# Mish feed-forward layer on one core: the first product of three row blocks done jointly on one weight load

## The chip, the core and the metric

The kernel runs on one core of one Trainium2 chip. The metric is the device time of one execution in microseconds (us). Three runs give 104.45, 105.22 and 105.36 us; the median, 105.22 us, is the time before.

## What is computed

```python
def reference(x, w1, b1, w2):          # x [1, 2048, 512], w1 [512, 1792], w2 [1792, 512], bfloat16
    h = jnp.einsum("bsd,df->bsf", x, w1) + b1
    sp = jnp.log1p(jnp.exp(-jnp.abs(h))) + jnp.where(h > 0, h, jnp.zeros_like(h))
    act = h * jnp.tanh(sp)             # mish(h)
    return jnp.einsum("bsf,fd->bsd", act, w2)
```

## The kernel before

The 2048 rows of x are worked in four blocks of 512 rows (blocks 0 to 3, the index `s`). Each block goes through two products.

**First product** (`mm1`, with its matmuls in `mm1_step`, L176). For each of FT = 14 column tiles `f` of w1 (128 columns each), KT = 4 matmuls `k` accumulate 128 values of h by the 512 rows of the block in one bank of `ps`. The weights are the tile `w1_sb[:, k, f]`; the moving operand is `xT[:, k, rows of the block]`, x transposed. After the fourth matmul ScalarE's `mish` (L159) adds the bias, applies Mish and writes `a_sb[:, f, rows of the block]`.

**Second product** (`mm2`, with its matmuls in `mm2_step`, L198). For each output tile `i` of 128 rows (16 in all, four to a block), 14 matmuls accumulate 128 rows by 512 output columns in one bank. The weights are pieces of `a_sb`, the moving operand is w2. `put` lets VectorE copy the bank to `o_sb` (L204) and SP store it (L207). The last tile is done in two pieces, of 384 and 128 columns, and the second is stored from ScalarE's queue.

Each `nc.tensor.matmul` call is two instructions on TensorE: a weight load (LDWEIGHTS, on the row PEld of the profile) and the matmul (MATMUL, on the row PE).

`ps` has eight banks of 512 float32 columns. `free[bank]` holds the instruction that last read the bank (a copy or a mish); the first matmul into a bank waits for it. Semaphore waits already known to be fulfilled are left out by `Stream.wait`. In blocks 1 to 3 the first product rotates over banks 4 to 7 and the second over 0 to 3:

```python
for f in range(FT):
    mm1(s, f, 4 + f % 4)
for i in range(starts[s] // P, starts[s + 1] // P):
    if i < S // P - 1:
        mm2(i, 0, D, i % 4)
```

Block 0 is handled apart, because it runs while the weights arrive: half of its rows are transposed by TensorE, the matmuls of its first eight tiles `f` are split by rows and ordered by the arrival of w1, and its second product uses banks `(i + 2) % 4`. Eight matmuls on constants ahead of it keep TensorE running until the data is there. The transposed x of blocks 1 to 3 (`xT`) comes by three transposing transfers, the last of the loads on SP's queue; the stores of the output follow on the same queue. Blocks 1 to 3 then run one after another: first product, second product, next block. Every engine works its instructions in the order in which they are written.

Of the kernel before, what the change touches and what calls it, by code (L numbers as in the profile page):

```python
# [5 lines left out]
P = 128  # L6
SQ = 32
WARM = (512,) * 5 + (256,) * 2 + (128,)
BLOCKS = (512, 512, 512, 512)
# [23 lines left out]
def bass_standalone__dense_activation_mish__prompt_kernel(  # L33
# [12 lines left out]
    _, S, D = x.shape  # L46
    F = w1.shape[1]
    KT, FT = D // P, F // P
# [4 lines left out]
    starts = [sum(BLOCKS[:i]) for i in range(len(BLOCKS) + 1)]  # L53
    OPEN = 8
    N0 = BLOCKS[0] // P

    with ExitStack() as es:
        def sb(name, shape, t):
            return es.enter_context(nc.sbuf_tensor(name, shape, t))

        x_nat = sb("x_nat", [P, 2, D], BF)
        xT = sb("xT", [P, KT, S], BF)
        w1_sb = sb("w1_sb", [P, KT, F], BF)
# [8 lines left out]
        ps = es.enter_context(nc.psum_tensor("ps", [P, 8, 512], F32))  # L72

        def sem(name):
            return es.enter_context(nc.semaphore(name))

        sp = Stream(nc.sync, None)
        pe = Stream(nc.tensor, sem("c_pe"))
        dve = Stream(nc.vector, sem("c_dve"))
        act = Stream(nc.scalar, sem("c_act"))  # L80
# [42 lines left out]
        for s in range(1, len(BLOCKS)):  # L123
            lo, hi = starts[s], starts[s + 1]
# [31 lines left out]
        def mish(s, f, bank, t_mm):  # L156
            n = BLOCKS[s]
            act.wait(t_b1c, t_mm)
            t = act.mark(act.eng.activation(a_sb[:, f, starts[s]:starts[s + 1]], ps[:, bank, 0:n], ACT.Mish,  # L159
                                            bias=b1_sb[:, f:f + 1]))  # L160
            t_mish[s, f] = t
            free[bank] = [t]

        def mm1_step(s, f, k, bank, js=None):

            n = BLOCKS[s]
            lo, hi = (0, n) if js is None else (js[0] * P, (js[-1] + 1) * P)
            first = k == 0 and lo == 0
            if first:
                pe.wait(*free[bank])  # L170
            pe.wait(t_w1[k, f])
            if s:
                pe.wait(t_xT[s])
            else:
                pe.wait(*[t_cp[j, k] for j in (js or range(N0))])
            return nc.tensor.matmul(ps[:, bank, lo:hi], w1_sb[:, k, f * P:(f + 1) * P],  # L176
                                    xT[:, k, starts[s] + lo:starts[s] + hi], start=first, stop=(k == KT - 1 and hi == n))

        def mm1(s, f, bank):
            for k in range(KT):  # L180
                mm = mm1_step(s, f, k, bank)
            mish(s, f, bank, pe.mark(mm))
# [10 lines left out]
        def mm2_step(i, f, lo, hi, bank):  # L193
            s = max(b for b in range(len(BLOCKS)) if starts[b] <= i * P)
            if f == 0:
                pe.wait(*free[bank])
            pe.wait(t_w2[f], t_mish[s, f])
            return nc.tensor.matmul(ps[:, bank, 0:hi - lo], a_sb[:, f, i * P:(i + 1) * P], w2_sb[:, f, lo:hi],  # L198
                                    start=(f == 0), stop=(f == FT - 1))

        def put(i, lo, hi, bank, t_mm, q=sp):
            nonlocal n_out
            dve.wait(t_mm)
            t = dve.mark(nc.vector.tensor_copy(o_sb[:, i, lo:hi], ps[:, bank, 0:hi - lo]))  # L204
            free[bank] = [t]
            q.wait(t)
            q.eng.dma_start(rows(i)[:, lo:hi], o_sb[:, i, lo:hi]).then_inc(s_out, 16)  # L207
            n_out += 1

        def mm2(i, lo, hi, bank, q=sp):  # L210
            for f in range(FT):
                mm = mm2_step(i, f, lo, hi, bank)
            put(i, lo, hi, bank, pe.mark(mm), q)
# [3 lines left out]
        def first(fs, js, ks, last=False):  # L217
            for k in ks:
                for f in fs:
                    mm = mm1_step(0, f, k, (4 + f) % 8, js)  # L220
                    if last and k == KT - 1:
                        mish(0, f, (4 + f) % 8, pe.mark(mm))
# [19 lines left out]

        for i in range(N0):
            mm2(i, 0, D, (i + 2) % 4)
        for s in range(1, len(BLOCKS)):
            for f in range(FT):
                mm1(s, f, 4 + f % 4)
            for i in range(starts[s] // P, starts[s + 1] // P):
                if i < S // P - 1:
                    mm2(i, 0, D, i % 4)  # L250
                else:
                    mm2(i, 0, D - P, i % 4)
                    mm2(i, D - P, D, (i + 1) % 4, act)
        sp.eng.wait_ge(s_out, 16 * n_out)


# [26 lines left out]
```

## Time and profile before

| | |
|---|---|
| median of three runs | 105.22 us (104.45 to 105.36) |
| time of the profiled execution | 104.7 us |
| its span, first to last instruction | 103.4 us |
| TensorE matmuls (PE) busy | 100.3 us, 97% of the span |
| TensorE weight loads (PEld) busy | 49.0 us, 47% |
| ScalarE (ACT) busy | 39.2 us, 38% |
| VectorE (DVE) busy | 13.3 us, 13% |
| mean granted TensorE clock | 1.000 |

The profile is of one execution. Its timelines give an instruction's start (us from the start of the span), its duration, engine, line and operation, then what it writes and reads, the shape and a count; in brackets stands the idle time of the engine just before, and what ended it. A row can merge several instructions of one kind, and its duration is then that of the whole stretch. Groups of instructions give busy time and mean duration (ns), then idle time before them. The windows give the busy time of each engine within a stretch, with the number of instructions, then the granted clock, the DMA engines' share and GB/s. Matmuls overlap their successors, so the duration of one (379 ns at 512 columns) is longer than the step from one to the next. A few matmul records are missing from the trace. The profile shortens names: `w_sb` is w1_sb or w2_sb, `b_sb` is b1_sb.

### The profile page before, as it was taken

What the parts mean: (1) busy time and instruction counts of PE and PEld (TensorE: products, weight loads), DVE (VectorE), ACT (ScalarE), POOL (GpSimd) and SP (SyncE); (2) the same over time, 40 slices, a digit from 0 to 9 for tenths busy, and PEclk for the clock granted to TensorE, in tenths of its full rate; (3) what the DMA queues carried; (4) which work ended last, traced back from release to release, by engine and by line L of the source; (5) the groups of instructions that cost most, each with busy time, mean ns of one, the idle gap of its engine ahead of it and who ended that gap; (6) DMA issues with size and microseconds to landing.
All of it is one profiled execution on the core that took longest, in us unless ns stands there. A gap on an engine that the chain in (4) does not pass through costs nothing.

```text
span 103.4 us, 1142 instructions
## 1 busy us (share of the span) xinstructions
PE 100.3 (97%) x497; PEld 49.0 (47%) x506; DVE 13.3 (13%) x26; ACT 39.2 (38%) x59; POOL 0.4 (0%) x5
## 2 busy tenths in 40 slices
PE   7999999999999999999999999999999999999992
PEld 2788444444444444444444444444444444444462
DVE  1212000211220000022220000022201000020223
ACT  4300999100037777100007777400006777700000
POOL 1000000000000000000000000000000000000000
PEclk9999999999999999999999999999999999999999
DMA  2999999991110000011011000001111000001111
GB/s 40 390 276 370 361 240 207 200 206 51 51 51 0 0 0 6 0 51 50 1 51 51 0 0 3 6 0 51 51 51 51 0 0 0 0 0 57 51 51 51
DMA packets 12833, 7.94 MB, mean 77 GB/s; under 512 B 7836, under 2 KB 12188, under 8 KB 12828
## 3 DMA queue, kind: packets, MB, share of 16 engines
q1 hardware_dynamic: 12396, 7.31, 27.0%
q10 hardware_dynamic: 432, 0.56, 1.5%
q8 instruction: 4, 0.07, 0.3%
q14 instruction: 1, 0.01, 0.0%
HBM read 3.94 MB, written 2.10 MB: 58 GB/s over the span
## 4 chain that ended last, share of the span: by engine, by line
PE 97%; issue 1%; DVE 0%
PE ps L176 47%; PE ps L198 47%; PE ps L105 3%; PE ps L145 1%; DVE o_sb L204 0%
## 5 line engine op out<-in xcount | busy, mean ns | idle before, releaser
L159 ACT ACTIVATE a_sb<-ps,b_sb 128x512 bf16<-128x512 f32 x56 | 37.1, 697 | 47.8 <-PE ps L176 42.8
L176 PE MATMUL ps<-xT,w_sb 128*128 128x512 bf16 (+2 forms) x247 | 48.8, 356 | 0.3
L198 PE MATMUL ps<-w_sb,a_sb 128*128 128x512 bf16 (+2 forms) x234 | 48.8, 366 | 0.2
L176 PEld LDWEIGHTS ps<-xT,w_sb 128*128 128x128 bf16 x252 | 24.4, 99 | 23.9
L198 PEld LDWEIGHTS ps<-w_sb,a_sb 128*128 128x128 bf16 x238 | 22.8, 98 | 25.9
L204 DVE CAST o_sb<-ps 128x512 bf16<-128x512 f32 (+2 forms) x17 | 11.2, 660 | 82.1 <-PE ps L198 82.1
L105 PE MATMUL ps<-const-bfloat16-1.0 128*128 128x512 bf16 (+2 forms) x8 | 2.8, 535 | 0.8 <-PEq L268 0.8
L105 PEld LDWEIGHTS ps<-const-bfloat16-1.0 128*128 128x128 bf16 x8 | 1.0, 140 | 2.2 <-issue 2.1
L150 ACT ACTIVATE xT<-ps 128x128 bf16<-128x128 f32 (+1 forms) x2 | 0.9, 438 | 2.4 <-PE ps L145 2.4
L107 ACT ACT_TABLE_LOAD x1 | 1.3, 1283 | 0.7 <-PEq L268 0.7
L228 DVE STREAM_TRANSPOSE b_T<-b_nat 32x32 bf16<-32x32 bf16 x4 | 0.8, 202 | 2.9 <-DMA b_nat<-in_b_dram 2.8
L150 DVE CAST xT<-ps 128x128 bf16<-128x128 f32 (+1 forms) x2 | 0.7, 358 | 2.6 <-PE ps L145 2.6
L145 PE MATMUL ps<-ident,x_nat 128*128 128x128 bf16 x8 | 1.0, 308 | 0.0
L145 PEld LDWEIGHTS ps<-ident,x_nat 128*128 128x128 bf16 x8 | 0.8, 138 | 0.4 <-DMA x_nat<-in_x_dram 0.4
L130 DVE TENSOR_SCALAR ident<-diff 128x128 bf16<-128x128 int32 x1 | 0.2, 226 | 0.2 <-POOL diff L128 0.2
L128 POOL IOTA diff<- 128x128 int32 x1 | 0.2, 235 | 0.4 <-POOLq L268 0.4
L102 DVE MEMSET b_nat<- 32x64 uint32 x1 | 0.1, 112 | 0.8 <-PEq L268 0.8
L230 DVE CAST b_sb<-b_T 128x14 f32<-128x14 bf16 x1 | 0.2, 176 | 0.0
L268 POOL MEMSET const-uint8-127<- 128x1 uint8 x1 | 0.1, 103 | 0.0
L268 POOL MEMSET const-bfloat16-1.0<- 128x1 bf16 x1 | 0.1, 102 | 0.0
L268 POOL MEMSET const-float32-0.0<- 128x1 f32 x1 | 0.1, 99 | 0.2 <-issue 0.2
L268 POOL MEMSET const-float32-1.0<- 128x1 f32 x1 | 0.1, 99 | 0.0
## 6 DMA issues: line engine op xcount, KB each, us to landing
out_dram<-o_sb SPq DMA_DIRECT2D x15, 128.0 KB, 1.7
w_sb<-in_w_dram SPq DMA_DIRECT2D x1, 1792.0 KB, 10.5
w_sb<-in_w_dram SPq DMA_DIRECT2D x1, 768.0 KB, 5.8
w_sb<-in_w_dram ACTq DMA_DIRECT2D x2, 256.0 KB, 3.8
w_sb<-in_w_dram SPq DMA_DIRECT2D x2, 256.0 KB, 3.6
x_nat<-in_x_dram SPq DMA_DIRECT2D x1, 256.0 KB, 2.8
out_dram<-o_sb SPq DMA_DIRECT2D x1, 96.0 KB, 1.6
xT<-in_x_dram SPq DMA_TRANSPOSE x4, 5.2
```

Source lines behind the costliest of these rows:

```text
L105: t_fill = [pe.mark(nc.tensor.matmul(ps[:, 7, 0:n], c_w, c_m[:, 0:n], start=True, stop=True)) for n in WARM]
L107: act.eng.preload_act_table(ACT.Mish)
L128: t_diff = pool.mark(pool.eng.iota(diff[:, :], pattern=[[1, P]], base=0, channel_multiplier=-1))
L130: t_id = dve.mark(nc.vector.tensor_scalar(ident[:, :], diff[:, :], 0, None, ALU.is_equal))
L145: mm = nc.tensor.matmul(ps[:, bank, lo:lo + P], x_nat[:, j, k * P:(k + 1) * P], ident[:, :], start=True, stop=True)
L150: t = eng.mark(nc.vector.tensor_copy(dst, src) if eng is dve else act.eng.activation(dst, src, ACT.Copy))
L159: t = act.mark(act.eng.activation(a_sb[:, f, starts[s]:starts[s + 1]], ps[:, bank, 0:n], ACT.Mish, bias=b1_sb[:, f:f + 1]))
L176: return nc.tensor.matmul(ps[:, bank, lo:hi], w1_sb[:, k, f * P:(f + 1) * P], xT[:, k, starts[s] + lo:starts[s] + hi], start=first, stop=( ...
L198: return nc.tensor.matmul(ps[:, bank, 0:hi - lo], a_sb[:, f, i * P:(i + 1) * P], w2_sb[:, f, lo:hi], start=(f == 0), stop=(f == FT - 1))
L204: t = dve.mark(nc.vector.tensor_copy(o_sb[:, i, lo:hi], ps[:, bank, 0:hi - lo]))
L228: t = dve.mark(nc.vector.transpose(b1_T[j * SQ:(j + 1) * SQ, :], b1_nat[:, j * SQ:(j + 1) * SQ]))
L268: nc = _bacc.Bacc("TRN2", target_bir_lowering=False, num_devices=1)
```

## The change

Blocks 1 to 3 no longer run one after another. Their first products run jointly: for each `f` and each `k`, three matmuls follow each other, one for each block, on the same weight tile `w1_sb[:, k, f]`. The first of them loads the weights; the other two are written by the new `matmul_loaded` as a MATMUL without a LDWEIGHTS. Three banks are accumulated at a time, taken in rotation from all eight: bank `(3 f + s - 1) % 8`. Three mish follow for each `f`. Only then comes the second product, all twelve output tiles in a row, on banks `(i + 2) % 4`, as block 0's.

```diff
--- before.py
+++ after.py
@@ -161,7 +161,15 @@
             t_mish[s, f] = t
             free[bank] = [t]
 
-        def mm1_step(s, f, k, bank, js=None):
+        def matmul_loaded(out, w, v, start, stop):
+
+            eng = nc.tensor
+            return eng.add_instruction(mybir.InstMatmult(
+                start_tensor_calc=start, stop_tensor_calc=stop, tile_size=(P, P), tile_position=(0, 0), ldweights=False,
+                name=nc.get_next_instruction_name(), engine=eng.engine,
+                ins=[eng.lower_ap(v), eng.lower_ap(w)], outs=[eng.lower_ap(out)]))
+
+        def mm1_step(s, f, k, bank, js=None, loaded=False):
 
             n = BLOCKS[s]
             lo, hi = (0, n) if js is None else (js[0] * P, (js[-1] + 1) * P)
@@ -173,8 +181,9 @@
                 pe.wait(t_xT[s])
             else:
                 pe.wait(*[t_cp[j, k] for j in (js or range(N0))])
-            return nc.tensor.matmul(ps[:, bank, lo:hi], w1_sb[:, k, f * P:(f + 1) * P],
-                                    xT[:, k, starts[s] + lo:starts[s] + hi], start=first, stop=(k == KT - 1 and hi == n))
+            return (matmul_loaded if loaded else nc.tensor.matmul)(
+                ps[:, bank, lo:hi], w1_sb[:, k, f * P:(f + 1) * P], xT[:, k, starts[s] + lo:starts[s] + hi],
+                start=first, stop=(k == KT - 1 and hi == n))
 
         def mm1(s, f, bank):
             for k in range(KT):
@@ -242,15 +251,21 @@
 
         for i in range(N0):
             mm2(i, 0, D, (i + 2) % 4)
-        for s in range(1, len(BLOCKS)):
-            for f in range(FT):
-                mm1(s, f, 4 + f % 4)
-            for i in range(starts[s] // P, starts[s + 1] // P):
-                if i < S // P - 1:
-                    mm2(i, 0, D, i % 4)
-                else:
-                    mm2(i, 0, D - P, i % 4)
-                    mm2(i, D - P, D, (i + 1) % 4, act)
+        rest = range(1, len(BLOCKS))
+        for f in range(FT):
+            banks = {s: (len(rest) * f + s - 1) % 8 for s in rest}
+            for k in range(KT):
+                t_mm = {s: mm1_step(s, f, k, banks[s], loaded=(s > 1)) for s in rest}
+                if k == KT - 1:
+                    t_mm = {s: pe.mark(t_mm[s]) for s in rest}
+            for s in rest:
+                mish(s, f, banks[s], t_mm[s])
+        for i in range(N0, S // P):
+            if i < S // P - 1:
+                mm2(i, 0, D, (i + 2) % 4)
+            else:
+                mm2(i, 0, D - P, (i + 2) % 4)
+                mm2(i, D - P, D, (i + 3) % 4, act)
         sp.eng.wait_ge(s_out, 16 * n_out)
```

On TensorE's queue, at the passage from block 0's second product to what follows, there stands before (L198 is the second product, L176 the first; `s_xT1` is the arrival of block 1's transposed x, `c_act` a mish, `c_dve` a copy by VectorE):

```order
L198 MATMUL ps<-w_sb,a_sb 128x512 [waits c_act] x7
L198 MATMUL ps<-w_sb,a_sb 128x512 x42
L176 MATMUL ps<-xT,w_sb 128x512 [waits s_xT1]
L176 MATMUL ps<-xT,w_sb 128x512 x15
L176 MATMUL ps<-xT,w_sb 128x512 [waits c_act]
```

The same place on TensorE's queue now (L207 is the second product, L184 a matmul of the first product with its load, L167 one without):

```order
L207 MATMUL ps<-w_sb,a_sb 128x512 [waits c_act] x7
L207 MATMUL ps<-w_sb,a_sb 128x512 x42
L184 MATMUL ps<-xT,w_sb 128x512 [waits s_xT1,c_dve]
L167 MATMUL ps<-xT,w_sb 128x512 [waits s_xT2,c_dve]
L167 MATMUL ps<-xT,w_sb 128x512 [waits s_xT3]
L184 MATMUL ps<-xT,w_sb 128x512
L167 MATMUL ps<-xT,w_sb 128x512 x2
```

The first two matmuls of the joint part now wait for VectorE's copies of block 0's tiles 2 and 3 (banks 0 and 1), where the matmul of block 1 waited for no copy; and all three blocks of x are waited for here.

Inside the joint part, from the tile `f` = 3 on, TensorE's queue holds for each `f` three waits on mish, two of them at matmuls that load nothing:

```order
L184 MATMUL ps<-xT,w_sb 128x512 [waits c_act]
L167 MATMUL ps<-xT,w_sb 128x512 [waits c_act] x2
L184 MATMUL ps<-xT,w_sb 128x512
L167 MATMUL ps<-xT,w_sb 128x512 x2
L184 MATMUL ps<-xT,w_sb 128x512
L167 MATMUL ps<-xT,w_sb 128x512 x2
```

Before, there was one such wait for each `f` of a block, always at a matmul with its load.

## The prediction

> **What bounds the kernel now.** I read the page's busy times and chain first, then the groups of instructions, then the timeline of TensorE alone.
>
> ```profile
> span 103.4 us, 1142 instructions
> PE 100.3 (97%) x497; PEld 49.0 (47%) x506; DVE 13.3 (13%) x26; ACT 39.2 (38%) x59; POOL 0.4 (0%) x5
> PEclk9999999999999999999999999999999999999999
> ...
> PE 97%; issue 1%; DVE 0%
> ...
> L176 PE MATMUL ps<-xT,w_sb 128*128 128x512 bf16 (+2 forms) x247 | 48.8, 356 | 0.3
> L198 PE MATMUL ps<-w_sb,a_sb 128*128 128x512 bf16 (+2 forms) x234 | 48.8, 366 | 0.2
> L176 PEld LDWEIGHTS ps<-xT,w_sb 128*128 128x128 bf16 x252 | 24.4, 99 | 23.9
> L198 PEld LDWEIGHTS ps<-w_sb,a_sb 128*128 128x128 bf16 x238 | 22.8, 98 | 25.9
> ```
>
> TensorE's matmuls are 97% of the chain that ended last, at the full granted clock. The two product lines (L176, the first product; L198, the second) have 0.3 and 0.2 us of idle time before them in all. So the end moves only if the matmuls follow each other faster, or if they are made to wait. The weight loads, 49.0 us of busy time, lie in a row of their own (PEld) that overlaps PE; whether they take any of the matmuls' time is the first question. The timeline of TensorE gives the pace:
>
> ```profile
> 16.71 12.25 PE L198 MATMUL ps<-w_sb,a_sb 128*128 128x512 bf16 x55
> 28.80 12.25 PE L176 MATMUL ps<-xT,w_sb 128*128 128x512 bf16 x55
> 40.88 12.25 PE L198 MATMUL ps<-w_sb,a_sb 128*128 128x512 bf16 x55
> ```
>
> Each row is 56 matmuls in the program (one record is missing in each). From 16.71 to 40.88 us there are 112 of them: 24.17 / 112 = 0.2158 us each, in both products alike, and no gap where one product passes to the other. That passage is the second thing to look at, because the change makes it anew at 28.80 us.
>
> **Loads: 112 are removed.** In blocks 1 to 3 the first product has 14 x 4 weight tiles, used by three blocks: 168 loads become 56. What a load costs the matmuls shows where matmuls are short: the last output tile is done in a piece of 384 columns and then one of 128, and VectorE's copy of each starts when its matmuls end.
>
> ```profile
> 100.77 0.56 DVE L204 CAST o_sb<-ps 128x384 bf16<-128x384 f32 x1 [1.58 <-PE ps L198]
> 101.55 0.29 DVE L204 CAST o_sb<-ps 128x128 bf16<-128x128 f32 x1 [0.23 <-PE ps L198]
> ```
>
> Between the two starts lie the 14 matmuls of 128 columns, each with a load of its own: 0.78 / 14 = 56 ns for a matmul with its load, although a load's record lasts 98 ns. So loads are hidden and pipelined even there. Going from 128 to 512 columns adds 215.8 - 56 = 160 ns for 384 columns, 0.416 ns a column; 512 columns are then 213.1 ns, and 2.7 ns are left for everything in a matmul and its load that does not grow with columns. That is the most a load can cost: 112 x 2.7 = 0.30 us. The least is nothing. I take nothing, because every load starts with the matmul before its own and has 216 ns for its 98 (rows below: the load at 28.58, its matmul at 28.80). The page "TensorE: Matmul & The Clock Gate" of the Trainium skill, section "Wait — 56ns, not 53.3ns?", puts about 2.5 ns of a warm matmul down to a fixed cost of the matmul itself, which a removed load leaves in place: by it the gain is nothing, and if the remainder were the load's it would be 0.30 us; the trace has matmul and load only as pairs and cannot part them.
>
> The 56 loads that stay now stand behind two matmuls that need the weights before them. If such a load starts as late as the last of the three matmuls, it still has 216 ns for 98. I take nothing here too; the price without that cover is in the rivals.
>
> **The passage at 28.80 us: a new wait.** Block 0's last output tile (tile 3) is accumulated in bank (3 + 2) % 4 = 1. Before, the matmul after it went to bank 4, idle for long. Now the three blocks take banks 0, 1, 2, and the matmul of block 2 is the second in the row: its bank is the one that VectorE is just emptying.
>
> ```profile
> 28.37 0.10 PEld L198 LDWEIGHTS ps<-w_sb,a_sb 128*128 128x128 bf16 x1
> 28.58 1.39 PEld L176 LDWEIGHTS ps<-xT,w_sb 128*128 128x128 bf16 x7
> 28.80 1.46 PE L176 MATMUL ps<-xT,w_sb 128*128 128x512 bf16 x6
> 29.00 0.69 DVE L204 CAST o_sb<-ps 128x512 bf16<-128x512 f32 x1 [2.33 <-PE ps L198]
> 29.72 0.33 SPq L207 DMA_DIRECT2D out_dram<-o_sb  x1
> 29.86 0.69 ACT L159 ACTIVATE a_sb<-ps,b_sb 128x512 bf16<-128x512 f32 x1 [11.37 <-PE ps L176]
> ```
>
> The first matmul, of block 1 in bank 0, runs at 28.80 as before (bank 0 was tile 2's, whose copy began at 25.98 and took as long). The second would start 0.216 us later, at 29.02. Tile 3's copy runs from 29.00 to 29.69. From the end of a copy to what it releases, this row shows 0.03 us (the store on the SP queue, at 29.72). On TensorE the only such place is early in the program, where the first product waits for a copied piece of x:
>
> ```profile
> 3.91 0.29 DVE L150 CAST xT<-ps 128x128 bf16<-128x128 f32 x1 [2.59 <-PE ps L145]
> ...
> 4.31 0.14 PEld L176 LDWEIGHTS ps<-xT,w_sb 128*128 128x128 bf16 x1
> ```
>
> That copy ends at 4.20 and the load behind it starts at 4.31: 0.11 us at most, since another matmul was still running. So the second matmul starts between 29.72 and 29.80, a stall of 0.70 to 0.78 us. I take 0.78, since the row of TensorE is nearer than SP's. Behind that matmul stands everything TensorE does to the end, block 3's matmul (bank 2, free since tile 0) first, and none of it has slack to give the time back: TensorE is the chain.
>
> **What the joint order asks of the others.** ScalarE (the mish on L159) now gets three banks at once every 12 matmuls: 12 x 0.2158 = 2.59 us, for 3 x 0.69 = 2.07 us of work, so it keeps up. A mish starts 0.42 us after the start of its last matmul: the row above has it at 29.86, and that matmul, the fourth from 28.80, started at 28.80 + 3 x 0.216 = 29.45. Eight banks in rotation of three: the tightest reuse is the bank of block 1 at tile f, taken again by block 3 at tile f + 2. Counting matmuls from the start of f, its last one is number 9, its mish ends at 9 x 0.216 + 0.42 + 0.69 = 3.05 us, and the reuse is number 26, at 5.61 us: 2.56 us of slack. If ScalarE's cover were gone (over 0.86 us a mish), each tile f would be late by the excess; the 0.69 us is far from it. At the other end, the second product's tile 4 needs the last mish of block 1, which starts 0.23 us before the joint part ends and is done 0.46 us after it; the thirteen matmuls ahead of its use take 2.8 us.
>
> All transposed blocks of x must be in place at 28.80 instead of at 28.80, 53 and 77 us. The windows show when the transfers are over:
>
> ```profile
> 21.00:23.00 2.00, 2.00 (x11) 0.91 (x10) 0.04 (x1) 0.00 (x0) 0.00 (x0) 1.00 1.10 262
> 23.00:24.00 1.00, 1.00 (x6) 0.46 (x5) 0.65 (x1) 0.00 (x0) 0.00 (x0) 1.00 0.00 1
> ```
>
> The last two columns are the DMA engines' share and GB/s: busy up to 23 us, then nothing (the next are stores). So there are 5.8 us in hand. Cover gone, each microsecond of lateness past that would be one of stall. The SP queue's order is unchanged; the second product's twelve stores follow each other every 14 x 0.2158 = 3.02 us, as four in a row did before, and land long before the next:
>
> ```profile
> out_dram<-o_sb SPq DMA_DIRECT2D x15, 128.0 KB, 1.7
> ```
>
> The tail, 384 and 128 columns and the store from ScalarE's queue, is the same instructions in the same order; only the bank numbers differ.
>
> **Sum.** Loads 0 (-0.30 to 0), passage +0.78 (+0.70 to +0.78), ScalarE, transfers, stores and tail 0: +0.78, bounds +0.40 to +0.78. On the profiled execution: span 103.4 + 0.78 = 104.2 us, time 104.7 + 0.78 = 105.5 us. The profiled time lies 0.5 us below the median of the runs, 105.22; that median gives 106.0. The four times (104.45, 104.7, 105.22, 105.36) have the mean 104.93, and I predict from it: **105.7 us**. A change under 1% (1.05 us) is about what a measurement of this kernel cannot tell from none.
>
> **Rivals.**
> *Loads exposed (slower).* If a load may be pulled ahead of only its own matmul's predecessor when that one has a load too, or cannot start until the last matmul that uses the old weights has drained, the 56 remaining loads stand in the row: 56 x 98 ns = 5.5 us, so 105.7 + 5.5 = 111.2 us. It decides from the point where a load starts later than 118 ns into the third matmul. For it: no load in this trace stands behind a matmul without one. Against: the load quoted above starts a whole matmul (0.22 us) before its own, and lasts less than half of that. 5%.
> *Waits on matmuls (slower).* A matmul without a load carries its own wait for a bank. 23 of them do in the joint part. Until now these waits stood at loads, 0.1 us ahead. If a wait that is long fulfilled costs TensorE 0.03 to 0.11 us as the two releases above do, that is 0.7 to 2.5 us: 106.4 to 108.2 us. Against: matmuls in the first product are paced alike where their loads wait and where they don't. 9%.
> *Loads cost array time (faster).* If a load and a matmul could not overlap, the 112 loads would give back 112 x 98 ns = 11.0 us: 105.7 - 11.0 = 94.7 us. Against it stand 56 ns a pair, under the 98 of the load alone. 2%. The same page of the Trainium skill, Part 3, "The mechanism", says that loads overlap running matmuls only where the row groups differ, which they do not here; the trace disagrees, with loads beside matmuls in one full-array stream at 215.8 ns.
> *No stall, or loads worth the full 0.30.* The stall is hidden by something I have not seen, or the program keeps its loads and only the passage counts: between 104.6 (no stall, 0.30 gained) and 105.7. 14%.
> *Forecast*: 70%.
>
> **Range.** The low end is the fastest run with the least sum, 104.45 + 0.40 = 104.85, say 104.9. The high end takes in the cheaper half of the waits: 105.7 + 1.5 = 107.2. Left out are the exposed loads, the free loads and the dearest waits, about 1 in 8. Faster by over 1%: 2% from free loads and 2% from runs that scatter, 4%. Slower by over 1%: exposed loads 5%, waits 9%, and of the forecast's 70% the sixth part in which run scatter (0.9 us between the runs shown) lifts 0.74% over 1%, 11%: together 25%. Within 1%: 71%.
>
> **What would show it.** Loads recorded: 506 - 112 = 394. TensorE's idle time before the load-less line 0.7 us or so, put down to VectorE's copy, in one place at 29.1 us; after it 0.2158 us a matmul (a pace of 0.213 would say the 2.7 ns were the load's; one of 0.25 in the joint part alone, exposed loads). The joint part ends at 28.80 + 0.78 + 168 x 0.2158 = 65.8 us with mish in threes, 0.69 us each. The chain of waits holds the VectorE copy of tile 3 with 0.7%. The forecast is wrong if the copy's release does not hold the second matmul, or if steps of 12 matmuls take more than 2.6 us.

## The result and the profile after

The change makes the kernel slower by about 0.8%: 105.79 us median (105.08 to 106.34, 11 runs) against 104.86 us (104.42 to 105.36, 11 runs), ratio 1.008, 95% interval 1.0051 to 1.011. The forecast was 105.7 us, with a range of 104.9 to 107.2 and most of the chance (71%) on a change within 1%.

The page of the changed kernel, in the lines that answer to those shown of before:

```profile
span 104.6 us, 1041 instructions
PE 101.4 (97%) x506; PEld 38.5 (37%) x394; DVE 13.3 (13%) x26; ACT 36.2 (35%) x59; POOL 0.4 (0%) x5
...
PE 97%; DVE 1%; issue 0%
PE ps L207 46%; PE ps L184 24%; PE ps L167 23%; PE ps L105 3%; PE ps L145 1%; DVE o_sb L213 1%
...
L207 PE MATMUL ps<-w_sb,a_sb 128*128 128x512 bf16 (+2 forms) x238 | 48.7, 366 | 0.0
L184 PE MATMUL ps<-xT,w_sb 128*128 128x512 bf16 (+2 forms) x140 | 34.2, 344 | 0.0
L167 PE MATMUL ps<-xT,w_sb 128*128 128x512 bf16 x112 | 33.3, 379 | 0.6 <-DVE o_sb L213 0.6
```

The 112 loads are gone: 394 remain of 506, and PEld's busy time fell from 49.0 to 38.5 us. Nothing of those 10.5 us shows in the end. TensorE is still 97% of the chain, and a new piece has come into it, VectorE's copy of block 0's tile 3: 0.70 us from 29.53 us on, most of the 1% of L213 (the copy at the tail was there before). Of the matmuls of the two products only those without a load (L167) have idle time before them, 0.6 us, ended by that copy.

The timeline at the passage from block 0 to the joint part:

```profile
29.11 0.10 PEld L184 LDWEIGHTS ps<-xT,w_sb 128*128 128x128 bf16 x1
29.33 0.38 PE L184 MATMUL ps<-xT,w_sb 128*128 128x512 bf16 x1
29.53 0.69 DVE L213 CAST o_sb<-ps 128x512 bf16<-128x512 f32 x1 [2.33 <-PE ps L207]
30.25 0.33 SPq L216 DMA_DIRECT2D out_dram<-o_sb  x1
30.27 0.59 PE L167 MATMUL ps<-xT,w_sb 128*128 128x512 bf16 x2 [0.57 <-DVE o_sb L213]
30.49 0.10 PEld L184 LDWEIGHTS ps<-xT,w_sb 128*128 128x128 bf16 x1 [1.28 <-issue]
30.70 0.38 PE L184 MATMUL ps<-xT,w_sb 128*128 128x512 bf16 x1
```

The second matmul starts 0.94 us after the first instead of 0.22: it was held until the copy of bank 1 ended at 30.22, and started 0.05 us later. That is a stall of 0.73 us (0.72 by these two rounded rows, 0.73 by the whole joint part below; the bracket says 0.57, since it counts from the end of the first matmul's record). After it the matmuls follow each other as they did before the change; the end of the joint part shows it:

```profile
65.67 0.38 PE L184 MATMUL ps<-xT,w_sb 128*128 128x512 bf16 x1
65.88 0.59 PE L167 MATMUL ps<-xT,w_sb 128*128 128x512 bf16 x2
66.31 36.46 PE L207 MATMUL ps<-w_sb,a_sb 128*128 128x512 bf16 x182
```

From 29.33 to 66.31 are 36.98 us for 168 matmuls: 168 x 0.2158 = 36.25, and 0.73 over.

The two profiled spans differ by 1.2 us, more than 0.73. The rest lies ahead of the change, in instructions that it does not touch. The row of block 0's first product before the change, and that row and the next one after it:

```profile
4.41 12.46 PE L176 MATMUL ps<-xT,w_sb 128*128 128x128 bf16 x83
```

```profile
4.42 12.98 PE L184 MATMUL ps<-xT,w_sb 128*128 128x128 bf16 x84
17.24 12.25 PE L207 MATMUL ps<-w_sb,a_sb 128*128 128x512 bf16 x56
```

Block 0's second product starts at 17.24 us here and at 16.71 in the execution of before; 0.53 us are lost between 4.4 us and there. In the profiles of the experiments, one for each kernel, in which this part is the same too, it starts anywhere from 16.4 to 17.5 us. So this part scatters without the change; what causes it was not tried. A comparison of two profiled spans would have put 0.5 us too much down to the change.

### The profile page after: what moved, and what is told of

It is laid out like the page before. It is cut to its first block, busy times and chain, and to the rows that moved or that the text cites. A ratio compares the mean times of both kernels' runs of the same rounds, so it can differ in the third digit from the quotient of the medians.

```text
span 104.6 us, 1041 instructions
## 1 busy us (share of the span) xinstructions
PE 101.4 (97%) x506; PEld 38.5 (37%) x394; DVE 13.3 (13%) x26; ACT 36.2 (35%) x59; POOL 0.4 (0%) x5
## 4 chain that ended last, share of the span: by engine, by line
PE 97%; DVE 1%; issue 0%
PE ps L207 46%; PE ps L184 24%; PE ps L167 23%; PE ps L105 3%; PE ps L145 1%; DVE o_sb L213 1%
## 5 line engine op out<-in xcount | busy, mean ns | idle before, releaser
L207 PE MATMUL ps<-w_sb,a_sb 128*128 128x512 bf16 (+2 forms) x238 | 48.7, 366 | 0.0
L159 ACT ACTIVATE a_sb<-ps,b_sb 128x512 bf16<-128x512 f32 x56 | 34.0, 696 | 28.6 <-PE ps L184 28.6
L184 PE MATMUL ps<-xT,w_sb 128*128 128x512 bf16 (+2 forms) x140 | 34.2, 344 | 0.0
L167 PE MATMUL ps<-xT,w_sb 128*128 128x512 bf16 x112 | 33.3, 379 | 0.6 <-DVE o_sb L213 0.6
L207 PEld LDWEIGHTS ps<-w_sb,a_sb 128*128 128x128 bf16 x238 | 22.8, 98 | 26.4 <-issue 0.5
L184 PEld LDWEIGHTS ps<-xT,w_sb 128*128 128x128 bf16 x140 | 13.9, 102 | 35.2 <-issue 31.0
L213 DVE CAST o_sb<-ps 128x512 bf16<-128x512 f32 (+2 forms) x17 | 11.2, 660 | 83.3 <-PE ps L207 83.3
```

Of the source, the lines that this page charges most:

```text
L167: return eng.add_instruction(mybir.InstMatmult(start_tensor_calc=start, stop_tensor_calc=stop, tile_size=(P, P), tile_position=(0, 0), ldw ...
L184: return (matmul_loaded if loaded else nc.tensor.matmul)(ps[:, bank, lo:hi], w1_sb[:, k, f * P:(f + 1) * P], xT[:, k, starts[s] + lo:start ...
```

## The experiments

The theory: the whole loss is the wait for one bank, and loads cost the matmuls nothing. The rivals: the joint order or the waits carried by matmuls cost time all along; or the removed loads did give something, which the stall hides.

**Other banks.** The joint part opens in banks 4, 5 and 6.

```diff
-            banks = {s: (len(rest) * f + s - 1) % 8 for s in rest}
+            banks = {s: (len(rest) * f + s + 3) % 8 for s in rest}
```

> The change with its banks moved on by four, (3 f + s + 3) % 8, so that the joint part opens in banks 4, 5, 6, long free. If the wait for VectorE's copy of tile 3 is the whole cost (theory): no idle time of TensorE at the passage, the joint part paced at 0.2158 us a matmul, time as before, ratio to before 1.000 within 0.003. If the joint order or the waits carried by the matmuls without a load cost the time (rival): still about 0.7 us slower, ratio 1.006 or more. If the loads removed gave time that the stall hid: under before, down to 0.30 us, ratio 0.997.

Measured: 104.75 us median, ratio to before 0.9995 (0.9963 to 1.0028). Its timeline at the passage:

```profile
28.86 0.38 PE L184 MATMUL ps<-xT,w_sb 128*128 128x512 bf16 x1
29.06 0.69 DVE L213 CAST o_sb<-ps 128x512 bf16<-128x512 f32 x1 [2.33 <-PE ps L207]
29.08 0.59 PE L167 MATMUL ps<-xT,w_sb 128*128 128x512 bf16 x2
...
65.12 36.46 PE L207 MATMUL ps<-w_sb,a_sb 128*128 128x512 bf16 x179
```

The second matmul starts 0.22 us after the first, beside the copy, and the joint part takes 65.12 - 28.86 = 36.26 us, 168 x 0.2158. The loss is gone with the bank. Joint order, the 23 waits on a mish at matmuls without a load, and 56 loads behind matmuls without one cost nothing together.

**The loads back, the banks as changed.**

```diff
-                t_mm = {s: mm1_step(s, f, k, banks[s], loaded=(s > 1)) for s in rest}
+                t_mm = {s: mm1_step(s, f, k, banks[s], loaded=False) for s in rest}
```

> The change in its order and with its banks, but every matmul loads its weights (168 loads in the joint part in place of 56). Theory, loads are free: as the change, stall 0.73 us, 0.2158 us a matmul, ratio to before 1.008. If a removed load is worth the 2.7 ns: 112 x 2.7 ns = 0.30 us slower than the change, ratio 1.011.

Measured: 105.81 us median, ratio to before 1.009 (1.0059 to 1.0122). That is near the change's own result, but the interval holds both 1.008 and 1.011, so the timeline decides:

```profile
29.19 0.38 PE L184 MATMUL ps<-xT,w_sb 128*128 128x512 bf16 x1
30.14 36.22 PE L184 MATMUL ps<-xT,w_sb 128*128 128x512 bf16 x163 [0.57 <-DVE o_sb L213]
66.20 36.46 PE L207 MATMUL ps<-w_sb,a_sb 128*128 128x512 bf16 x179
```

The stall is there with 168 loads as with 56: 30.14 - 29.19 - 0.22 = 0.73 us. The load of the waiting matmul was held with it and starts when the matmul does:

```profile
30.14 1.41 PEld L184 LDWEIGHTS ps<-xT,w_sb 128*128 128x128 bf16 x8 [1.06 <-DVE o_sb L213]
```

So this one load has no matmul ahead to hide behind. Still, from 29.19 to 66.20 are 37.01 us against 36.98 with 56 loads, 0.03 us more at most.

**Both edits**, so that of the change only the joint order is left.

> Both: banks moved on by four and every matmul with its load, so of the change only the joint order is left. Theory: as before, ratio 1.000 within 0.003, no idle time at the passage. If the joint order itself costs: above 1.005.

Measured: 105.02 us median, ratio 1.0022 (0.9988 to 1.0057), which by itself excludes neither nothing nor 0.30 us. Again the timeline decides:

```profile
29.08 36.42 PE L184 MATMUL ps<-xT,w_sb 128*128 128x512 bf16 x164
65.34 36.46 PE L207 MATMUL ps<-w_sb,a_sb 128*128 128x512 bf16 x179
```

65.34 - 29.08 = 36.26 us with 168 loads, and 36.26 us with 56 in the first experiment. The 0.30 us at which a removal of the loads was bounded would be thirty times the resolution of these rows; it is not there.

**The busy bank third instead of second.**

```diff
+            if f == 0:
+                banks = {1: 0, 2: 2, 3: 1}
```

> The change, but for the first tile f block 2 takes bank 2 and block 3 bank 1, so that the busy bank comes third instead of second. Theory: the copy of tile 3 ends at the same moment, and one matmul more runs ahead of it: stall 0.73 - 0.22 = 0.51 us, ratio to before about 1.005. If the delay came from something else at the passage (the arrival of x, the waits' number), the stall stays 0.73 us.

Measured: 105.46 us median, ratio 1.0054 (1.002 to 1.0088).

```profile
29.12 0.38 PE L184 MATMUL ps<-xT,w_sb 128*128 128x512 bf16 x1
29.32 0.69 DVE L213 CAST o_sb<-ps 128x512 bf16<-128x512 f32 x1 [2.33 <-PE ps L207]
29.34 0.38 PE L167 MATMUL ps<-xT,w_sb 128*128 128x512 bf16 x1
30.04 0.33 SPq L216 DMA_DIRECT2D out_dram<-o_sb  x1
30.07 0.38 PE L167 MATMUL ps<-xT,w_sb 128*128 128x512 bf16 x1 [0.35 <-DVE o_sb L213]
```

The second matmul, in bank 2, is on time; the third waits for the copy and starts 0.73 us after the second instead of 0.22, a stall of 0.51 us. The stall ends with the copy and shrinks by what runs ahead of it, so the arrival of x and the number of waits are out.

**What a load costs where matmuls are short.** In four kernels, built on the one with other banks, each matmul of the joint part is cut into pieces of 128 or of 64 columns. In one of each pair every piece loads its weights; in the other the first of the 12 or 24 pieces on a weight tile loads them. A third pair with 32 columns followed when these had shown no difference.

```diff
+            for c in range(lo, hi, 128 if s else hi - lo):
+                d = min(hi, c + (128 if s else hi - lo))
+                mm = (matmul_loaded if loaded or c > lo else nc.tensor.matmul)(
+                    ps[:, bank, c:d], w1_sb[:, k, f * P:(f + 1) * P], xT[:, k, starts[s] + c:starts[s] + d], ...
```

128 columns, with all loads and with one:

> As the change with banks moved on by four, but each matmul of the joint part is cut into four of 128 columns, each with its own load (672 matmuls, 672 loads). Theory: 56 ns a pair as in the last output tile of before, joint part 672 x 0.056 = 37.6 us against 36.3 us.

> The same four pieces of 128 columns, but only the first of the twelve matmuls on a weight tile loads it (672 matmuls, 56 loads). If the 2.7 ns that do not grow with columns are the matmul's: 56 ns each, 37.6 us, as with all loads. If they are the load's: 53.3 ns each, 35.8 us.

64 columns:

> Pieces of 64 columns, each with its own load (1344 of both). Alone, such a matmul should take 64 x 0.416 + 2.7 = 29.3 ns. If loads are free at any width: 29.3 ns, joint part 39.4 us. If a load has a least step of its own, it shows here, at some value up to the 56 ns known from 128 columns: up to 75 us.

> Pieces of 64 columns, one load for 24 matmuls (1344 matmuls, 56 loads). Matmul alone: 29.3 ns, 39.4 us; more, if TensorE cannot issue matmuls so fast. The difference to the kernel with all loads is what removing loads is worth at this width.

32 columns:

> Pieces of 32 columns, each with its own load (2688 of both in the joint part). By the line through the wider ones a matmul is 32 x 0.416 + 2.7 = 16.0 ns, joint part 43.0 us. At 64 columns a load went with every 29 ns and cost nothing; if its own step lies between 16 and 29 ns it shows here: up to 78 us.

> Pieces of 32 columns, one load for 48 matmuls. 43.0 us if matmuls follow each other at 16.0 ns; longer if TensorE has a least step for matmuls alone. Where this and the kernel with all loads take the same time, loads are free at 32 columns too; where they differ, the difference over 2632 loads is the price of one.

Measured, one execution each; the joint part runs from its first matmul to the first of the second product in TensorE's timeline:

| columns | loads in the joint part | time | joint part | step of a matmul |
|---|---|---|---|---|
| 128 | 672 | 106.23 us | 29.06 to 66.58: 37.52 us | 55.8 ns |
| 128 | 56 | 106.2 us | 29.02 to 66.54: 37.52 us | 55.8 ns |
| 64 | 1344 | 108.48 us | 29.62 to 68.82: 39.20 us | 29.2 ns |
| 64 | 56 | 108.32 us | 29.45 to 68.65: 39.20 us | 29.2 ns |
| 32 | 2688 | 145.15 us | 29.16 to 105.50: 76.34 us | 28.4 ns |
| 32 | 56 | 135.31 us | 28.46 to 95.66: 67.20 us | 25.0 ns |

In the four kernels of 128 and 64 columns the record of the second product's first matmul is missing, so the first one recorded is the second, and the table takes its step of 0.22 us off. The sign of it is VectorE's copy of tile 4, which starts when that tile's 14 matmuls end. With all loads, at 64 and at 32 columns:

```profile
72.05 0.69 DVE L216 CAST o_sb<-ps 128x512 bf16<-128x512 f32 x1 [41.53 <-PE ps L210]
108.72 0.69 DVE L216 CAST o_sb<-ps 128x512 bf16<-128x512 f32 x1 [78.66 <-PE ps L210]
```

The first starts 3.01 us after the first recorded matmul of the second product (69.04, below), the other 3.22 us after it (105.50). At 64 columns, 1344 loads and 56 take the same time. The rows of TensorE with all loads:

```profile
29.62 39.36 PE L186 MATMUL ps<-xT,w_sb 128*128 128x64 bf16 x1344
69.04 36.24 PE L210 MATMUL ps<-w_sb,a_sb 128*128 128x512 bf16 x178
```

and the group of its loads:

```profile
L186 PEld LDWEIGHTS ps<-xT,w_sb 128*128 128x128 bf16 x1428 | 47.9, 99 | 4.6
```

A load's record lasts 99 ns and one goes with every 29 ns, so on average more than three are under way at a time. The step without a load is that with one. The steps at 64, 128 and 512 columns (29.2, 55.8 and 215.8 ns) lie on one line of 0.417 ns a column with 2.5 ns on top, so the 2.5 ns are the matmul's and not the load's. So says the page "TensorE: Matmul & The Clock Gate" of the Trainium skill, section "Wait — 56ns, not 53.3ns?", which puts about 2.5 ns down to the matmul itself.

At 32 columns the two differ for the first time, but in pauses, not in the step. The rows of the loads, where every matmul has one:

```profile
28.95 11.68 PEld L186 LDWEIGHTS ps<-xT,w_sb 128*128 128x128 bf16 x450
40.81 3.27 PEld L186 LDWEIGHTS ps<-xT,w_sb 128*128 128x128 bf16 x128 [0.18 <-issue]
44.82 3.27 PEld L186 LDWEIGHTS ps<-xT,w_sb 128*128 128x128 bf16 x128 [0.73 <-issue]
48.27 3.27 PEld L186 LDWEIGHTS ps<-xT,w_sb 128*128 128x128 bf16 x128 [0.18 <-issue]
52.00 3.27 PEld L186 LDWEIGHTS ps<-xT,w_sb 128*128 128x128 bf16 x128 [0.46 <-issue]
```

From the 450th load on, TensorE pauses after every 128 pairs of load and matmul. A row of 3.27 us is 127 steps of 25.0 ns and the last load's 0.10 us, so between the pauses the step is the partner's. 128 pairs at that step take 3.20 us; but the rows from 40.81 us on start 4.01, 3.45 and 3.73 us apart, so these pauses are 0.81, 0.25 and 0.53 us. The wait list of this kernel gives them no releaser but "issue":

```profile
PEld ps L186 <- issue: 7.7, 18, 0.7
```

What TensorE lacks there was not settled. One candidate, argued and not tested, is the supply of instructions. The DMA queue for instructions moved 21 packets (0.34 MB) between 29 and 105 us, one for every 128 pairs, which are 256 instructions; the partner, with half the instructions, needed 11 packets in about as long and does not pause. At 64 columns with all loads it is 10 packets in 40 us, also without a pause.

The partner's own step is 25.0 ns, where the line through the wider matmuls gives 15.8. It has one load for 48 matmuls, so that step is not set by the loads.

## Why the prediction was right

**The passage**, the one term of the sum, was taken at 0.78 us and measured at 0.73. What was off is the release: 0.05 us from the copy's end to the matmul on TensorE, between the 0.03 of the SP queue and the 0.11 of the early load, where I had taken the latter. Two experiments show the cause, not only the place: another bank takes the whole of it away, and a matmul ahead of the wait takes away its own 0.22 us. It was never given back, as forecast: both rows of the second product that follow last 36.46 us, in the change as in the kernel with other banks.

**The loads** were taken at nothing, with a bound of 0.30 us: 36.26 us for the joint part with 168 loads and with 56. The argument from the last tile's 128 columns (56 ns a pair, under a load's 98) held, and goes down to 64 columns. The 2.7 ns of the bound came from rows rounded to 0.01 us; the finer steps give 2.5 ns, and all of it stays when the load goes.

**ScalarE, transfers, stores and tail** cost nothing, and ScalarE had more room than stated: three mish of a tile take 1.84 us in a row, not 3 x 0.69 = 2.07.

```profile
63.49 1.84 ACT L159 ACTIVATE a_sb<-ps,b_sb 128x512 bf16<-128x512 f32 x3 [0.75 <-PE ps L184]
66.08 1.84 ACT L159 ACTIVATE a_sb<-ps,b_sb 128x512 bf16<-128x512 f32 x3 [0.75 <-PE ps L184]
```

The records of mish following each other overlap, so the duration of one is not its step. The last three start at 66.08 us, 0.23 before the second product, as worked out.

**The rivals.** Exposed loads did not occur: the load for the matmul at 30.70 starts at 30.49, with the last of the three matmuls that use the old weights, and has 0.1 us in hand. Their price of 98 ns each was too high as well, as far as one case tells: the load that started with its matmul in the second experiment lengthened the joint part by 0.03 us at most. Waits at matmuls cost nothing: in the first experiment 23 of them lie in 36.26 us that are 168 steps to the hundredth. Loads that take the array's time are refuted by the pairs at 29.2 ns. The rule of the same page of the Trainium skill, Part 3, "The mechanism", that loads overlap matmuls only in other row groups, does not hold here: the trace has them side by side in full-array matmuls. The same section also names a background weight buffer as a case in which loads are pulled ahead, which the prediction left out; no run here can show whether that is what is seen.

**The size.** 104.93 + 0.78 gave 105.7; measured 105.79. The base was good to 0.1 us (104.86 over eleven runs), and the difference of the medians, 0.93 us, is wider than the 0.73 of the trace by no more than its interval (1.0051 to 1.011 of 104.86 us is 0.53 to 1.15 us). That the forecast lies within 0.1 us of the measured median is in part luck: 104.86 + 0.73 is 105.59, and the 0.2 us from there to 105.79 lie within the interval, and no trace explains them. The prediction also held that a change under 1% is about what a measurement cannot tell from none; with eleven runs of each kernel the interval of the ratio leaves out 1.

## What to carry to other kernels

Before removing weight loads, divide a stretch of the timeline by its matmuls, at the narrowest matmul there is: if the step grows with the columns alone, the loads are hidden, as here, where a PEld row at 47% of the span was worth nothing. When an order is rewritten on an engine that is the chain, look at the first use of every buffer behind the seam: a rotation of banks that is right in its steady run can begin on the one bank that is still being read, and here that 0.7 us was the whole effect. Take the loss from the place in the trace, not from the difference of two profiled spans.

## What the runs showed of the hardware

Weight loads of 128 x 128 bfloat16 ran several deep: their records last 96 to 99 ns in the mean, and they went with matmuls every 55.8, 29.2 and, between the pauses, 25.0 ns without lengthening the step. The step was 2.5 ns and 0.417 ns a column from 64 to 512 columns, with loads and without. At 32 columns matmuls came no closer than 25.0 ns, even with one load for 48 of them. With 2688 pairs of load and matmul at that step TensorE paused 18 times for up to 0.8 us, and the joint part took 9.1 us longer than with 56 loads. From the end of VectorE's copy to the matmul that waited for its bank it took 0.05 us.
